# First chunk of an mLSTM kernel: another order of its pieces, smaller first feed-forward units, a weight quarter narrowed in halves, no spare products

## The chip, the cores and the metric

The kernel runs on one NeuronCore of a Trainium2 chip. The metric is the device time of one execution in microseconds (us), the median over executions; lower is better. The core has a matrix engine (PE, with its weight loads shown apart as PEld), a vector engine (DVE), an activation engine (ACT), a third elementwise engine (POOL), and a queue that issues most transfers (SP). Each engine works through its own list of instructions in order, and waits on counters (semaphores) that other engines raise.

## The reference

Two blocks follow each other. The first is an mLSTM cell over 4 batches, 8 heads, 768 steps, head size 40:

```python
for t in range(S):
    m_new = np.maximum(f_gate[:, :, t] + m, i_gate[:, :, t])
    f_stab = np.exp(f_gate[:, :, t] + m - m_new)
    i_stab = np.exp(i_gate[:, :, t] - m_new)
    C = f_stab * C + i_stab * einsum('bhd,bhe->bhde', vt, kt)
    n = f_stab * n + i_stab * kt
    h_tilde = einsum('bhde,bhe->bhd', C, qt)
    denom = max(abs(sum(n * qt)), 1.0)
    y[:, :, t] = sigmoid(o_gate[:, :, t]) * h_tilde / denom
```

Its output, as 3072 tokens of 320 values, goes through a feed-forward block with `w_in` of 320 x 2048 and `w_out` of 2048 x 320:

```python
h = x @ w_in
return np.maximum(0.01 * h, h) @ w_out
```

The two weights arrive as 64-bit floats and are narrowed to 32 bits on the chip.

## The kernel before, in words

The 768 steps are cut into 6 chunks of 128. Within a chunk the cell is computed without a loop over steps: scores of keys against queries, times a matrix of decays (`w`, the exponential of a masked sum), times values, plus a state that is carried from chunk to chunk. One *step* `s` is one batch in one chunk, `s = 4 * chunk + batch`, so chunk 0 holds s = 0 to 3 and chunk 1 holds s = 4 to 7. A chunk's four outputs are transposed into `xT`, and the feed-forward of that chunk (a *group*) runs on them while the next chunk's cell is worked out.

The feed-forward of group 0 comes in *units*. A first kind makes 2 x 128 of the 2048 hidden values from all 5 row blocks of `w_in` (`rows`, line 888) and applies the leaky ReLU on ACT (`relu`, 897). Pair `j` (0 to 7) needs quarter `j // 2` of `w_in`. A second kind, `part(n, m)` (923), multiplies a quarter `m` of the hidden values of batch `n` by `w_out`. In group 0 before the change, the first kind is cut in halves of two batches (`half`, 915), and units 0 and 1 belong to the first chunk's order; 14 halves and 16 parts follow, numbered 0 to 29. From group 1 on, a pair is one product over all four batches, cut in two units by row blocks (`pair`, 902).

`narrow_weights(n)` (235) is a generator of seven steps, one on ACT (the absolute value, line 246) and six on DVE (248 to 262). n = 0 to 3 are the quarters of `w_in`, 1280 columns each; n = 4 to 11 are eighths of `w_out`, 640 columns each.

The order of all this is written out by hand in two places, inside a context that keeps every engine's list as it was emitted:

- `ORDER` (1087) is a list for chunk 0. Its words are calls: `ld` loads k, q, v of a batch and `lo` its o gate; `lw` loads a piece of weights as raw 64-bit words; `g`, `ge`, `ug` are the gates of a chunk (scans on DVE, exponentials on ACT, transposes on PE); `tr` and `tc` transpose k or q on PE and copy them on ACT; `ab` and `abw` spread the gate sums over a matrix (PE) and add the mask (DVE, 456); `exp` is the exponential of `w` (ACT, 473); `vu` is v times a gate (POOL, 483); `sc` and `scm` the scores (PE, 578) and their product with `w` (DVE, 585); `st` and `stc` the state (PE, 593) and its copy (DVE, 601); `val` the values (PE, 658); `den` the denominators (DVE, 650 to 652); `o` the gate's tanh (ACT, 509); `gate` the gating (DVE, 670); `gp` the scaling (POOL, 687); `x` and `xc` the transposes to `xT` (PE, 861) and their copies (ACT, 874 and 875); `ps` clears what a state buffer needs (POOL, 160 to 162); `tiles` clears others; `nw n` is one step of narrowing; `ff` a feed-forward unit; `fd` and `ll` load for chunk 1. `warm 12` is 12 products of the identity with itself, whose result nobody reads.
- After that list, a loop over the 30 units of group 0 (1154). `PASSES[i]` says how many further steps of narrowing (w_in's third quarter onward) stand ahead of unit i; `fetch` at which unit the last pieces of `w_out` are asked for; `place` after which unit each of chunk 1's 13 cell pieces stands: the scores (`u_parts`, PE 635 and 640, DVE 645 and 617) and the outputs (`u_plain`, PE 698, DVE 650 to 709, POOL 687) of s = 4, 5, 6, one gate transpose, the same two of s = 7, and four times `u_x1`, the transposes of s = 4 to 7 into `xT` with their copies.

Then comes the first unit of group 1, which reads all four batches of `xT`. The buffers of products are two sets of four banks (`psf` for the feed-forward, the gate sums and `warm`; `psc` for the cell).

Of the kernel before, what the change touches and what calls it, by code (L numbers as in the profile page):

```python
# [20 lines left out]
def kernel(  # L21
# [27 lines left out]
    B, H, S, D = q.shape  # L49
    P = 128  # L50
# [15 lines left out]
    NF = FF // P  # L66
    GT = B * P
    KF = Dm // P
    KR = Dm - KF * P
    KC = Dm // DP  # L70
# [4 lines left out]
    gp = ctx.enter_context(tc.tile_pool(name="gates", bufs=1))  # L75
# [96 lines left out]
    def f_of(r, j):  # L172
        n, e = divmod(j, 2)
        return 4 * n + 2 * r + e

    def w_row(r, slot, j):
        n, e = divmod(j, 2)
        at = (2 * slot + e) * P
        return w_in[DP * r : DP * (r + 1), n, at : at + P]
# [3 lines left out]
    raws = {}  # L183
# [48 lines left out]
            rows = moe_w_out[2 * m * P : 2 * (m + 1) * P, :]  # L232
            nc.sync.dma_start(to.rearrange("p (a d) -> p a d", d=Dm), rows.rearrange("(a p) d -> p a d", p=P))

    def narrow_weights(n):

        if not wide:
            return  # L240
        raw, dst = raws.pop(n)
        words = raw.bitcast(U32).rearrange("p (c two) -> p c two", two=2)
        lo, hi = words[:, :, 0], words[:, :, 1]
        d = dst.bitcast(U32)
        low, top = lo.bitcast(F32), hi.bitcast(F32)
        nc.scalar.activation(dst, top, AF.Abs)
        yield
        nc.vector.tensor_scalar(
            dst, dst, scalar1=2.0**-15, scalar2=122879.9921875, op0=ALU.max, op1=ALU.min,
        )  # L250
        yield
        nc.vector.tensor_scalar(
            d, d, scalar1=0x07FFFFFF, scalar2=3, op0=ALU.bitwise_and, op1=ALU.logical_shift_left,
        )
        yield
        nc.vector.scalar_tensor_tensor(d, in0=hi, scalar=0xC0000000, in1=d, op0=ALU.bitwise_and, op1=ALU.bitwise_or)  # L256
        yield
        nc.vector.tensor_scalar(hi, d, scalar1=0xFF800000, scalar2=None, op0=ALU.bitwise_and)
        yield
        nc.vector.scalar_tensor_tensor(low, in0=lo, scalar=2.0**-52, in1=top, op0=ALU.mult, op1=ALU.mult)  # L260
        yield
        nc.vector.tensor_tensor(dst, dst, low, op=ALU.add)  # L262
# [78 lines left out]
    st = {}  # L341
# [540 lines left out]
    def by_slot(t, dt=F32):  # L882
        return t[:].bitcast(dt).rearrange("p b (k t) -> p k b t", t=P)

    def ff_units(g):
        xT = by_slot(st["xT", g])

        def rows(j, ph, cols, slots):
            bs = slice(cols.start // P, cols.stop // P)
            for slot in slots:  # L890
                for r in range(2):
                    nc.tensor.matmul(  # L892
                        ph[r][:, cols], lhsT=w_row(r, slot, j), rhs=xT[DP * r : DP * (r + 1), slot, bs, :],
                        start=(slot == 0), stop=(slot == KC - 1),
                    )

        def relu(j, ph, cols):
            for r in range(2):
                f = f_of(r, j)
                nc.scalar.activation(acts[:, f, cols], ph[r][:, cols], AF.Prelu, alpha=0.01)  # L900

        def pair(j):
            ph = []

            def first():
                ph.extend(psf.tile([P, GT], F32, name=f"ph{r}", tag="mm") for r in range(2))
                rows(j, ph, slice(0, GT), range(3))

            def second():
                rows(j, ph, slice(0, GT), range(3, KC))  # L910
                relu(j, ph, slice(0, GT))

            return [first, second]

        def half(j, h):
            ph = [psf.tile([P, GT], F32, name=f"ph{r}", tag="mm") for r in range(2)]
            cols = slice(h * GT // 2, (h + 1) * GT // 2)
            rows(j, ph, cols, range(KC))
            relu(j, ph, cols)

        po = {}

        def part(n, m):
            if m == 0:
                po[n] = psf.tile([P, Dm], F32, name="po", tag="mm")
            for f in range(m * NF // 4, (m + 1) * NF // 4):
                nc.tensor.matmul(  # L927
                    po[n][:], lhsT=acts[:, f, ts(n, P)], rhs=w_out[:, f, :], start=(f == 0), stop=(f == NF - 1),
                )
            if m == 3:  # L930
                if n < 2:
                    y = wk.tile([P, Dm], F32, name="y")[:]
                else:
                    y = wk.tile([P, H, D1], F32, name="hn")[:].rearrange("p h d -> p (h d)")[:, :Dm]
                nc.scalar.copy(y, po[n][:])
                nc.sync.dma_start(out[n * S + g * P : n * S + (g + 1) * P, :], y)

        if g == 0:

            ins = [(j, h) for j0 in range(0, NF // 2, 2) for h in range(2) for j in (j0, j0 + 1)]  # L940
            return [lambda j=j, h=h: half(j, h) for j, h in ins] + [
                lambda n=n, m=m: part(n, m) for m in range(4) for n in range(B)
            ]
        firsts = [u for j in range(NF // 2) for u in pair(j)]
        for n in range(2):
            firsts[KH + 2 * n] = lambda n=n, u=firsts[KH + 2 * n]: (u(), mix_early(n))
        return firsts, fast_units(g)
# [5 lines left out]
    def mix_early(n):  # L953

        nc.vector.tensor_tensor(s3_at[:, n], quarter(n, 0, 0), quarter(n, 1, 0), op=ALU.subtract)
# [91 lines left out]
    def run(steps, n=None):  # L1047

        for _ in range(H if n is None else n):
            next(steps, None)  # L1050
# [34 lines left out]
            nc.tensor.matmul(st["warm"][:], lhsT=ident[:], rhs=ident[:], start=True, stop=True)  # L1085

    ORDER = """
ld 0; warm 12; ld 1; ld 2; lo 0; lo 1; lo 2; lw 0
g 0; ld 3; lw 1; lw 2; lo 3; ge 0; ug 0; tr 0 0
tr 0 1; vu 1; vu 0; tc 0 0; ab 0; abw 0; tr 1 0; tc 0 1  # L1090
exp 0; sc 0; abw 1; tr 1 1; tc 1 1; st 0; tc 1 0; exp 1
st 1; scm 0; stc 1; stc 0; ab 2; tiles; g 1; abw 3
sc 1; scm 1; ge 1; abw 2; val 0; tr 2 0; tr 2 1; val 1
o 1; den 0; tc 2 1; gate 1; ps 1; tc 2 0; o 0; exp 2
gate 0; gp 0; ug 1; sc 2; scm 2; x 0; tr 3 0; nw 0
nw 0; vu 2; den 1; gp 1; nw 0; nw 0; nw 0; exp 3
tr 3 1; tc 3 0; ps 0; st 2; tc 3 1; xc 0; val 2; vu 3
sc 3; stc 2; nw 0; o 2; nw 0; nw 1; scm 3; den 2
x 1; xc 1; gate 2; st 3; o 3; gp 2; nw 1; nw 1
stc 3; nw 1; ff 0; val 3; den 3; x 2; gate 3; fd 4  # L1100
nw 1; ps 3; xc 2; ff 1; gp 3; x 3; nw 1; ll 4 1
xc 3; ps 2; ll 4 2; fd 5; ll 5 1; lw 3; lw 4; lw 5
lw 6; fd 6; fd 7; ll 5 2; nw 1
"""

    def first_chunk():

        ffs, narrow = [], {}

        def ff(n):  # L1110
            if not ffs:
                ffs.extend(ff_units(0))
            ffs[n]()

        def step(n):
            if n not in narrow:
                narrow[n] = narrow_weights(n)
            next(narrow[n], None)

        acts_of = {  # L1120
            "ld": load, "lo": load_o, "lw": load_weights, "g": gates, "ge": gates_exp, "warm": warm,
            "ug": lambda c: gates_T(c, bus[c][0] if c == 0 else bus.pop(c)[0]),
            "tr": u_transpose, "tc": transpose_copy, "ab": lambda n: spread_first(bus[0][1], n), "abw": spread_mask,
            "exp": lambda n: run(prep_exp(n)), "vu": prep_vu, "tiles": prepare_tiles, "sc": u_scores, "scm": scores_mix,
            "st": state, "stc": state_copy, "val": u_values, "den": values_den, "o": prep_o, "gate": gate,
            "gp": gate_scale, "nw": step, "ps": prepare_step, "x": u_x, "xc": x_copy, "ff": ff,
            "warmer": warmer, "idle": idle, "fd": feed, "ll": load_late,
        }
        for line in ORDER.split("\n"):
            for what in line.split(";"):  # L1130
                name, *args = what.split() or [None]
                if name:
                    acts_of[name](*map(int, args))
        return ffs

    E = mybir.EngineType
    with tc.manual_schedule(engines={E.PE, E.DVE, E.Activation, E.Pool}):
        ffs = first_chunk()[2:]
        fetch = {6: (3, 4), 17: (7,), 10: (5, 6)}
        PASSES = (3, 2, 1, 0, 3, 5, 3, 1, 0, 1, 4, 2, 3, 4, 1, 2, 8, 4, 5, 4, 5, 4, 0, 7, 3, 5, 5, 1, 2, 8)  # L1140
        place = (1, 4, 7, 9, 11, 15, 15, 18, 23, 25, 27, 27, 28)
        late = {}
        now = (None for n in range(2, QN + NF // 2) for _ in narrow_weights(n))

        def exps():
# [8 lines left out]
        for i in range(len(ffs)):  # L1154
            run(now, PASSES[i])
            for n in fetch.get(i, ()):
# [102 lines left out]
        for g in range(1, NB):  # L1259
            firsts, seconds = three_units(g, 0) if g in THREE else ff_units(g)  # L1260
            ffs = firsts + seconds
# [51 lines left out]
```

## Time and profile before

| | before |
|---|---|
| median of 3 executions | 491.95 us (491.8 to 493.19) |
| the profiled execution | 493.52 us, span 491.7 us, mean granted clock 0.975 |
| PE busy in the span | 480.2 us (98%) |
| DVE busy | 371.4 us (76%) |
| ACT busy | 197.2 us (40%) |
| POOL busy | 164.2 us (33%) |
| PE busy, 0 to 137.5 us | 129.20 us, DVE 120.14 us, mean granted clock 0.91 |
| PE busy, 137.5 to 371.6 us | 234.10 of 234.10 us |
| PE busy, 371.6 to 491.7 us | 116.89 of 120.1 us |

The span goes from the first instruction to the last. Everything that the change edits lies in the first 137.5 us. The ORDER list ends on PE at 48.1 us (the last transposes of batch 3), the units run from 49.07 to 136.92, and group 1 begins at 137.50. A row of the profile names line, engine, operation, the tile written and the tile read; a fp32 product shows as two rows. The granted clock is the share of full speed at which PE was let run.

### The profile page before, as it was taken

Reading aid. Unit: us, or ns where it says so; the run is one execution under the profiler, and the core shown is the slowest. Engines: PE = TensorE matmul, PEld = TensorE weight load, DVE = VectorE, ACT = ScalarE, POOL = GpSimd, SP = SyncE. Lnnn points to the kernel's source line nnn. Section 1 sums busy time; section 2 is a strip of 40 time slices with the busy share of each in tenths; the row PEclk is TensorE's granted clock in tenths of the full one; section 3 lists DMA queues with packets and bytes.
Section 4 is the critical chain, followed back from the end, with each engine's and each line's share of the span. In section 5 each row is a group of like instructions: output and inputs, shape, how many; then the busy total and the mean of one; then the engine's idle time right before and its main releaser. Section 6 shows DMA issues by size and latency. Waiting matters only on the chain.

```text
span 491.7 us, 12838 instructions
## 1 busy us (share of the span) xinstructions
PE 480.2 (98%) x5137; PEld 381.7 (78%) x5137; DVE 371.4 (76%) x595; ACT 197.2 (40%) x510; POOL 164.2 (33%) x207
## 2 busy tenths in 40 slices
PE   7989998999999999999999999999999999999997
PEld 7877887777745479985549995557998889988997
DVE  5797999989943999777898677779899968335611
ACT  4773884562453241324333141425023752156310
POOL 5233664270410624827280472635220002100020
PEclk9757999999999999999999999999999999999999
DMA  7867777897434477668687867876161030100001
GB/s 139 186 192 135 209 176 137 247 226 155 102 122 88 115 156 184 166 143 202 138 190 159 193 164 174 180 174 172 35 237 42 1 107 1 41 15 0 1 1 54
DMA packets 142699, 63.41 MB, mean 129 GB/s; under 512 B 110832, under 2 KB 130864, under 8 KB 142640
## 3 DMA queue, kind: packets, MB, share of 16 engines
q1 hardware_dynamic: 142256, 62.47, 53.0%
q8 instruction: 40, 0.66, 0.6%
q10 hardware_dynamic: 384, 0.13, 0.1%
q14 instruction: 19, 0.16, 0.1%
HBM read 51.68 MB, written 8.27 MB: 122 GB/s over the span
## 4 chain that ended last, share of the span: by engine, by line
PE 79%; DVE 11%; SPq 3%; DMA 2%; issue 2%; ACT 1%; POOL 1%; DVEq 0%; POOLq 0%
PE po L968 31%; PE ph L892 23%; PE ph L818 8%; PE pe L818 4%; PE pT L728 3%; PE sd L635 3%; DMA S<-in_v_dram 1%; DVE raw L260 1%; SPq L228 1%; DVE w_out L262 1%; PE warm L321 1%; PE po L927 1%; PE sc L578 1%; PE sd L640 1%; DVE w_out L256 1%
## 5 line engine op out<-in xcount | busy, mean ns | idle before, releaser
L892 PE MATMUL ph<-xT,w_in 64*128 64x512 f32 (+1 forms) x800 | 146.8, 516 | 0.6 <-ACT xT L874 0.6
L892 PEld LDWEIGHTS ph<-xT,w_in 64*128 64x128 f32 x800 | 77.9, 190 | 58.1 <-issue 50.8
L968 PE MATMUL po<-w_out,acts 128*128 128x160 f32 x640 | 91.0, 301 | 0.0
L968 PEld LDWEIGHTS po<-w_out,acts 128*128 128x128 f32 x640 | 87.5, 190 | 3.4 <-ACT w L473 1.5
L900 ACT ACTIVATE acts<-ph 128x512 f32<-128x512 f32 (+1 forms) x80 | 36.8, 508 | 85.2 <-PE ph L892 85.2
L613 POOL TENSOR_TENSOR S<-S,f 40x336 f32<-40x336 f32 x36 | 33.6, 933 | 92.7 <-PE pT L728 49.0
L473 ACT ACTIVATE w<-w,gT 128x64 f32<-128x64 f32 (+1 forms) x192 | 52.0, 348 | 30.3 <-POOL w L465 29.2
L968 PE MATMUL po<-raw,acts 128*128 128x160 f32 x320 | 45.1, 299 | 0.0
L968 PEld LDWEIGHTS po<-raw,acts 128*128 128x128 f32 x320 | 44.0, 190 | 0.0
L1001 POOL TENSOR_TENSOR y<-y,raw 128x160 f32<-128x160 f32 x10 | 5.5, 555 | 112.3 <-ACT y L1000 112.3
L645 DVE TENSOR_TENSOR qn<-w,sd 64x512 f32<-64x512 f32 x40 | 27.4, 684 | 19.4 <-PE sd L640 13.0
L840 DVE SCALAR_TENSOR_TENSOR acts<-ph,acts 128x512 f32<-128x512 f32 x32 | 20.6, 685 | 20.7 <-ACT acts L838 20.7
L927 PE MATMUL po<-w_out,acts 128*128 128x320 f32 x128 | 36.1, 436 | 0.0
L465 POOL TENSOR_TENSOR w<-w,i 128x512 f32<-128x512 f32 x20 | 33.9, 1697 | 0.1
L526 DVE TENSOR_TENSOR qn<-kqT,ea 64x512 f32<-64x512 f32 x32 | 33.1, 1033 | 1.0
L927 PEld LDWEIGHTS po<-w_out,acts 128*128 128x128 f32 x128 | 23.7, 190 | 9.7 <-DVE w_out L262 0.4
L742 POOL TENSOR_TENSOR xb<-xb,den 128x320 f32<-128x320 f32 x16 | 11.6, 727 | 48.7 <-DVE xb L739 48.7
L838 ACT ACTIVATE acts<-pe 128x512 f32<-128x512 f32 x32 | 17.4, 594 | 19.2 <-PE pe L818 19.0
L746 DVE STREAM_TRANSPOSE x<-xb 128x512 f32<-128x512 f32 x16 | 17.7, 1107 | 7.7 <-POOL xb L742 7.7
L844 ACT ACTIVATE acts<-acts 128x512 f32<-128x512 f32 x32 | 19.7, 633 | 8.0 <-DVE acts L840 8.0
L968 PE MATMUL po<-raw 128*128 128x160 f32 x160 | 22.7, 300 | 0.0
L635 PEld LDWEIGHTS sd<-kqT 40*64 40x64 f32 x640 | 19.7, 135 | 3.7 <-issue 3.0
(164 smaller groups left out, 786.4 us busy)
## 6 DMA issues: line engine op xcount, KB each, us to landing
w<-a_dr SPq DMA_DIRECT2D x40, 128.0 KB, 3.6
rb<-in_k_dram SPq DMA_DIRECT2D x64, 80.0 KB, 2.7
rb<-in_q_dram SPq DMA_DIRECT2D x64, 80.0 KB, 2.7
rb<-in_o_gate_dram SPq DMA_DIRECT2D x64, 80.0 KB, 2.7
xT<-x_dr SPq DMA_DIRECT2D x32, 160.0 KB, 3.2
ea<-a_dr SPq DMA_DIRECT2D x32, 128.0 KB, 3.3
x_dr<-x SPq DMA_DIRECT2D x16, 256.0 KB, 3.2
kn<-in_k_dram SPq DMA_DIRECT2D x24, 160.0 KB, 3.4
```

Of the source, the lines that this page charges most:

```text
L465: nc.gpsimd.tensor_tensor(w, w, cm2.unsqueeze(1).to_broadcast([P, H, SL]), op=ALU.add)
L473: yield nc.scalar.activation(w[:, h, :], w[:, h, :], AF.Exp, bias=gT[c][:, 0, bh : bh + 1], scale=1.0)
L526: nc.vector.tensor_tensor(mixed(s)[rows, 1 - r], d["kqT"][rows, 1].rearrange("p (h t) -> p h t", t=SL), d["ea"][rows], op=ALU.mult,)
L613: nc.gpsimd.tensor_tensor(new, old, g, op=ALU.mult)
L635: nc.tensor.matmul(bank[1 - u][toks, h, :], lhsT=kqT[rows, 0, ts(h, SL)], rhs=kqT[rows, 1, ts(h, SL)], start=True, stop=True,)
L645: nc.vector.tensor_tensor(mixed(s)[toks, u], w[toks], bank[1 - u][toks], op=ALU.mult)
L818: nc.tensor.matmul(ph[r][:], lhsT=parts["w", key][n][part, at : at + P], rhs=xs[key][part, slot, :], start=start and slot == 0, stop=stop ...
L840: nc.vector.scalar_tensor_tensor(fs[r], in0=ph[r][:], scalar=1.0 + EPS, in1=fs[r], op0=ALU.mult, op1=ALU.add,)
L892: nc.tensor.matmul(ph[r][:, cols], lhsT=w_row(r, slot, j), rhs=xT[DP * r : DP * (r + 1), slot, bs, :], start=(slot == 0), stop=(slot == KC ...
L900: nc.scalar.activation(acts[:, f, cols], ph[r][:, cols], AF.Prelu, alpha=0.01)
L927: nc.tensor.matmul(po[n][:], lhsT=acts[:, f, ts(n, P)], rhs=w_out[:, f, :], start=(f == 0), stop=(f == NF - 1),)
L968: nc.tensor.matmul(bank[:], lhsT=left[:, f, :], rhs=right[:, f, :], start=f == 0, stop=f == KH - 1)
```

## The change

Four things change, all in chunk 0 and group 0.

1. `ORDER` is another list of the same pieces. Loads of the o gate, the gates, the transposes and the narrowing stand in other places, and `warm 12` is left out.
2. The first units are `some(j, b0, b1)`, over any run of batches. Before, ORDER held two halves: pairs 0 and 1 over batches 0 and 1. Now it holds pair 0 over batch 0, pair 0 over batch 1, and pair 1 over batches 0 and 1. Of the 30 units behind the list, units 0 and 1 are pairs 0 and 1 over batches 2 and 3, units 2 to 13 are pairs 2 to 7 over all four batches, each cut in two by row blocks as in later groups, and units 14 to 29 are the parts as before.
3. `narrow_weights(n, e)` can take half of a quarter: e = 0 is the columns of the even pair, e = 1 those of the odd one. ORDER narrows quarter 0 in these halves, 640 columns per step.
4. `PASSES`, `fetch` and `place` have other numbers. In `place` the last five pieces, the outputs of s = 7 and the four transposes into `xT`, all have unit 29, the last one.

```diff
-    def narrow_weights(n):
+    def narrow_weights(n, e=None):
...
+        if e is not None:
+            lo, hi, dst = (a.rearrange("p (k e t) -> p e k t", k=KC, t=P)[:, e] for a in (lo, hi, dst))
...
-        def half(j, h):
+        def some(j, b0, b1):
+
             ph = [psf.tile([P, GT], F32, name=f"ph{r}", tag="mm") for r in range(2)]
-            cols = slice(h * GT // 2, (h + 1) * GT // 2)
+            cols = slice(b0 * P, b1 * P)
...
-            ins = [(j, h) for j0 in range(0, NF // 2, 2) for h in range(2) for j in (j0, j0 + 1)]
-            return [lambda j=j, h=h: half(j, h) for j, h in ins] + [
-                lambda n=n, m=m: part(n, m) for m in range(4) for n in range(B)
-            ]
+            ins = [lambda j=j: some(j, 2, B) for j in range(2)] + [u for j in range(2, NF // 2) for u in pair(j)]
+            return some, ins + [lambda n=n, m=m: part(n, m) for m in range(4) for n in range(B)]
...
     ORDER = """
-ld 0; warm 12; ld 1; ld 2; lo 0; lo 1; lo 2; lw 0
-g 0; ld 3; lw 1; lw 2; lo 3; ge 0; ug 0; tr 0 0
-tr 0 1; vu 1; vu 0; tc 0 0; ab 0; abw 0; tr 1 0; tc 0 1
-exp 0; sc 0; abw 1; tr 1 1; tc 1 1; st 0; tc 1 0; exp 1
-st 1; scm 0; stc 1; stc 0; ab 2; tiles; g 1; abw 3
-sc 1; scm 1; ge 1; abw 2; val 0; tr 2 0; tr 2 1; val 1
-o 1; den 0; tc 2 1; gate 1; ps 1; tc 2 0; o 0; exp 2
-gate 0; gp 0; ug 1; sc 2; scm 2; x 0; tr 3 0; nw 0
-nw 0; vu 2; den 1; gp 1; nw 0; nw 0; nw 0; exp 3
-tr 3 1; tc 3 0; ps 0; st 2; tc 3 1; xc 0; val 2; vu 3
-sc 3; stc 2; nw 0; o 2; nw 0; nw 1; scm 3; den 2
-x 1; xc 1; gate 2; st 3; o 3; gp 2; nw 1; nw 1
-stc 3; nw 1; ff 0; val 3; den 3; x 2; gate 3; fd 4
-nw 1; ps 3; xc 2; ff 1; gp 3; x 3; nw 1; ll 4 1
-xc 3; ps 2; ll 4 2; fd 5; ll 5 1; lw 3; lw 4; lw 5
-lw 6; fd 6; fd 7; ll 5 2; nw 1
+ld 0; g 0; ld 1; lo 1; ge 0; lo 0; tr 0 0; ld 2
+lw 0; ug 0; tr 0 1; ab 0; tr 1 0; ld 3; tc 0 0; tc 0 1
+vu 0; sc 0; lw 1; tr 1 1; abw 0; abw 1; exp 0; lo 3
+vu 1; tc 1 1; st 0; st 1; tc 1 0; sc 1; tr 2 0; ab 2
+scm 0; val 0; tr 2 1; stc 1; exp 1; tiles; o 0; scm 1
+tc 2 1; lo 2; g 1; gate 0; vu 2; abw 2; lw 2; den 0
+vu 3; val 1; ge 1; abw 3; stc 0; o 1; st 2; ps 0
+tc 2 0; stc 2; ug 1; ps 1; nw 0 1; nw 0 0; exp 2; sc 2
+gp 0; tr 3 0; tr 3 1; nw 0 0; den 1; gate 1; tc 3 1; scm 2
+nw 0 1; tc 3 0; gp 1; nw 0 1; x 0; sc 3; exp 3; val 2
+xc 0; ps 2; nw 0 0; nw 0 0; nw 0 1; nw 0 0; x 1; nw 1
+o 2; nw 0 1; nw 0 0; nw 0 0; st 3; o 3; ff 0 0 1; scm 3
+nw 0 1; den 2; fd 4; ll 4 1; nw 1; val 3; gate 2; nw 0 1
+lw 3; lw 4; gp 2; xc 1; fd 5; nw 1; gate 3; ff 0 1 2
+ll 4 2; nw 1; den 3; nw 1; gp 3; x 2; nw 1; ll 5 1
+xc 2; stc 3; ff 1 0 2; x 3; lw 5; ps 3; nw 1; fd 6
+xc 3; fd 7; lw 6; ll 5 2
 """
...
-        fetch = {6: (3, 4), 17: (7,), 10: (5, 6)}
-        PASSES = (3, 2, 1, 0, 3, 5, 3, 1, 0, 1, 4, 2, 3, 4, 1, 2, 8, 4, 5, 4, 5, 4, 0, 7, 3, 5, 5, 1, 2, 8)
-        place = (1, 4, 7, 9, 11, 15, 15, 18, 23, 25, 27, 27, 28)
+        fetch = {10: (5, 6), 16: (7,), 4: (3, 4)}
+        PASSES = (6, 1, 2, 0, 1, 0, 4, 1, 0, 4, 3, 2, 9, 0, 1, 3, 11, 11, 1, 0, 5, 12, 2, 0, 2, 2, 2, 4, 0, 7)
+        place = (1, 5, 6, 9, 10, 12, 16, 20, 29, 29, 29, 29, 29)
```

The rest of the diff passes the new arguments through `ff` and `nw`.

More of the change, by code (lines that the diff above doesn't have):

```diff
@@ L233, in load_weights @@
             nc.sync.dma_start(to.rearrange("p (a d) -> p a d", d=Dm), rows.rearrange("(a p) d -> p a d", p=P))
-    def narrow_weights(n):
+    def narrow_weights(n, e=None):
         if not wide:
             return
-        raw, dst = raws.pop(n)
+        raw, dst = raws[n]
         words = raw.bitcast(U32).rearrange("p (c two) -> p c two", two=2)
         lo, hi = words[:, :, 0], words[:, :, 1]
+        if e is not None:
+            lo, hi, dst = (a.rearrange("p (k e t) -> p e k t", k=KC, t=P)[:, e] for a in (lo, hi, dst))
         d = dst.bitcast(U32)
@@ L1108, in first_chunk, with ff, step @@
         ffs, narrow = [], {}
-        def ff(n):
+        def ff(j, b0, b1):
             if not ffs:
                 ffs.extend(ff_units(0))
[L1113 to L1118, printed above, removed]
+            ffs[0](j, b0, b1)
+        def step(n, e=None):
+            if (n, e) not in narrow:
+                narrow[n, e] = narrow_weights(n, e)
+            next(narrow[n, e], None)
         acts_of = {
@@ L1133, in first_chunk @@
                     acts_of[name](*map(int, args))
-        return ffs
+        return ffs[1]
     E = mybir.EngineType
     with tc.manual_schedule(engines={E.PE, E.DVE, E.Activation, E.Pool}):
-        ffs = first_chunk()[2:]
-        fetch = {6: (3, 4), 17: (7,), 10: (5, 6)}
-        PASSES = (3, 2, 1, 0, 3, 5, 3, 1, 0, 1, 4, 2, 3, 4, 1, 2, 8, 4, 5, 4, 5, 4, 0, 7, 3, 5, 5, 1, 2, 8)
-        place = (1, 4, 7, 9, 11, 15, 15, 18, 23, 25, 27, 27, 28)
+        ffs = first_chunk()
+        fetch = {10: (5, 6), 16: (7,), 4: (3, 4)}
+        PASSES = (6, 1, 2, 0, 1, 0, 4, 1, 0, 4, 3, 2, 9, 0, 1, 3, 11, 11, 1, 0, 5, 12, 2, 0, 2, 2, 2, 4, 0, 7)
+        place = (1, 5, 6, 9, 10, 12, 16, 20, 29, 29, 29, 29, 29)
         late = {}
```

## The prediction

> **What bounds the kernel now.** I read the engine totals first, then busy time by stretch, since a share of the whole span mixes stages.
>
> ```profile
> PE 480.2 (98%) x5137; PEld 381.7 (78%) x5137; DVE 371.4 (76%) x595; ACT 197.2 (40%) x510; POOL 164.2 (33%) x207
> ```
>
> PE is nearly full. The change ends where chunk 1's feed-forward begins, so the stretches up to there count. The columns are stretch and length, then busy PE, PEld, DVE, ACT and POOL, granted clock, DMA share, GB/s.
>
> ```profile
> 8.97:46.23 37.26, 33.32 (x294) 28.81 (x295) 30.47 (x67) 22.90 (x61) 11.43 (x25) 0.68 0.79 176
> ...
> 51.30:128.07 76.77, 74.46 (x1079) 59.78 (x1075) 72.27 (x101) 42.38 (x112) 31.64 (x27) 1.00 0.80 189
> 49.07:136.92 87.85, 85.54 (x1137) 67.70 (x1130) 83.08 (x113) 51.30 (x133) 41.21 (x34) 1.00 0.76 178
> ```
>
> From the first unit that covers batches 2 and 3 (49.07) to chunk 0's last product (136.92) PE idles 87.85 - 85.54 = 2.31 us. DVE, which narrows the weights, idles 4.5 of 76.77 us. Two engines run close together, so an early start pays only if both have it. Before 49 us the waits and the clock count:
>
> ```profile
> 14.00:16.00 2.00, 2.00 (x34) 1.77 (x36) 1.88 (x7) 1.30 (x5) 0.00 (x0) 0.50 0.86 195
> 16.00:18.00 2.00, 2.00 (x25) 1.88 (x25) 1.86 (x8) 1.15 (x5) 0.00 (x0) 0.96 0.64 167
> 24.00:26.00 2.00, 2.00 (x16) 1.78 (x15) 0.63 (x2) 2.00 (x5) 1.30 (x3) 0.50 0.49 107
> 42.00:44.00 2.00, 2.00 (x14) 1.53 (x10) 0.33 (x1) 0.66 (x2) 0.00 (x0) 0.63 0.39 61
> ```
>
> PE runs at half clock from 13 to 16.6 and from 23.4 to 43.9 us. DVE's waits from 8 to 50 us:
>
> ```profile
> DVE den L650 <- PE pa L658: 2.7, 1, 2.7
> DVE w L456 <- PE ab L446: 2.0, 1, 2.0
> DVE w L585 <- PE sc L578: 1.6, 1, 1.6
> DVE S L601 <- PE dC L593: 0.9, 1, 0.9
> DVE x L670 <- PE pa L658: 0.7, 1, 0.7
> ```
>
> Last, the border to chunk 1, on ACT and PE (start, duration):
>
> ```profile
> 134.28 0.38 PE L861 MATMUL xt<-ident,hn 128*128 128x128 f32 x2
> ...
> 134.49 0.27 PE L862 MATMUL xt<-ident,hn 128*64 128x128 f32 x1
> ...
> 134.60 2.32 PE L927 MATMUL po<-w_out,acts 128*128 128x320 f32 x8
> ...
> 136.98 0.47 ACT L874 COPY xT<-xt 64x384 f32<-64x384 f32 x1
> 137.47 0.37 ACT L875 COPY xT<-xt 64x256 f32<-64x256 f32 x1
> ```
>
> Here PE transposes batch 3's x (`xt`) ahead of one more product, and ACT's copies pass partly beneath it. PE waits from 136.92 to 137.50, and its first unit of chunk 1 takes 5.01 instead of 4.49 us, being paced by the copies: 0.58 + 0.52 = 1.10 us.
>
> **The change, part by part.**
>
> *No spare products, other order: the start-up.* The 12 products (24 rows, 1.47 to 6.5) stand on nobody's path: `tg` needs ACT's `bu`, done at 6.45. What they do is raise the clock by the time work comes: four transposes at 8.82 take 0.66 us and at 26.29, at half clock, 1.06; 32 rows of `ab` take 1.17 at 7.71 and 2.09 at 13.73. At half clock `tg` also stands behind four transposes now; the first mask addition on DVE moves from 8.97 to about 10.1 (0.9 of `ab`, 0.2 of the transposes): +1.1.
>
> By the Trainium skill (TensorE: Matmul & The Clock Gate, "What's actually happening") the clock is halved by default and a busy window of about 3.4 us releases it. By that rule the removed products cost one such window, and the trace's 5 us of spare products before full clock agree; the 1.1 us above stands without it.
>
> DVE's work up to batch 3's denominators stays the same (`stc 3` moves behind them, `gate 3` ahead, 0.68 each) except for the halved narrowing of w_in's first quarter. Uncontended rows at 640 columns take 0.48, 0.49, 0.83, 0.49, 0.83, 0.82 (L248 to L262), 3.94 in sum; at 1280 columns 0.81, 0.78, 1.49, 0.81, 1.48, 1.49, or 6.86. Two halves: 7.88, so +1.0. On ACT two absolute values of 0.80 replace one of 1.39.
>
> DVE's five waits above total 7.9; the 2.0 is part of the start, 5.9 lie after 8.97. What is late next, followed through the new queues: `stc 1` behind the state products (0.35 to 1.15), `scm 1` behind `exp 1` (1.2), `gate 0` behind batch 0's values (0.1 to 1.35), `gate 3` behind batch 3's (0.6 to 2). The last is shorter than the 2.7, since 128-column units now stand ahead of these products in place of one of 256 columns (20 rows, 4.64 us at half clock). The low ends hold at full clock (values 1.98 for 16 rows), the high ends at half (3.64). Sum 2.25 to 5.7, against 5.9: -3.65 to -0.2. A 128-column unit has no row; it costs at most its 256-column one, 2.43 at full clock, at least half of that, and lies inside these waits.
>
> Start-up sum: 1.1 + 1.0 - 3.65 = -1.55, or 1.1 + 1.0 - 0.2 = +1.9. Following PE alone (units over batch 0, over batch 1, then both, behind these waits) gives -2.5 to +1.6. I take -0.2, nearer the half-clock end for the early part and the full-clock end for the late part: first full unit at 48.9.
>
> SP: `lo 1` and `lo 0` go ahead of `ld 2` (two issues of 0.87), which is not needed before 16. The first and second quarter are issued 0.87 sooner, the third 0.87 later. The fourth quarter's ten issues and w_out's first go ahead of `fd 5` and `ll 5`, some 7 us later for batch 1 of chunk 1, whose transposes come at 66. POOL: `vu 3` now waits for its load (landing about 24.4) ahead of `ps 0`, `ps 1` and `gp 0`; `x 0` on PE stands behind that, and `sc 3` behind `x 0`, at about 29, when `exp 3` is running anyway. These cost nothing while they hold; if the load is late, all of it shifts.
>
> *Units of chunk 0.* 512-column rows take 4.49 per 20, two halves 2 x 2.26: no change. Of PE's 2.31 idle, 0.74 + 0.97 at 79 to 81 (`hN` behind ACT and behind DVE's L617) goes: the second such product now follows unit 9, at about 77, and L617 is done by 75. Late next: the first `hN`, because L260 and L262 of the third quarter (3.0 to 3.8) go ahead of its L645; 0 to 0.5. And w_out: DVE's remaining work of 5.0 + 72.27 less the last cell's block, now behind (1.40 + 0.50 + 1.29 + 1.39 = 4.58), gives 72.7; with 4 of idle from about 46 this ends at 123, when PE reaches the last quarter of the products (48.9 + 83.1 - 9.1). Sum: -1.0; ends -2.0 and +1.5.
>
> *The border.* `place` puts the last cell's `hN` and all four transposes behind unit 29. PE's queue then reads: 36 products without a break, `hN` (1.06), four `xt` (0.33 each). Copies of one batch take 1.72 (132.36 to 134.08). First copy 1.06 + 0.52 (126.70 to 127.22) = 1.58 after the last product; the last batch's begins 3 x 1.72 = 5.16 later; its first is done at 7.21, and PE resumes at 7.26; pacing 0.52: 7.78. The last cell's gate (1.2 on DVE) and scale (0.74 on POOL) pass under the first three batches' copies. The 1.06 + 4 x 0.33 = 2.4 was done inside the 85.54 before, and 1.10 was lost: 7.78 - 2.4 - 1.10 = +4.3. Its cover was the products that used to follow each transpose. Nothing in the queues can shorten it; ends 4.0 and 4.6, plus the clock, below.
>
> **Sum.** -0.2 - 1.0 + 4.3 = +3.1. After the border PE's queue is the same, at full clock. The profiled execution took 493.52 (span 491.7), 1.57 above the median of 491.95: 496.6 against it, 495.05 against the median.
>
> **Rivals.**
> - *The start-up wins more than the border costs.* All of DVE's new waits at their low ends (PE at full clock by 10 us) and PE never waiting for w_out: -2.5 - 2.0 + 4.0 = -0.5. DVE with no wait at all would give 1.1 + 1.0 - 5.9 = -3.8, and -1.8 in sum: 490.2. It decides if full-size units begin before 46.3. For it: `o` loads come before the weights, where the trace shows ACT 2.7 late. Against it: half clock in 24 of the 37 us.
> - *A tie.* Start-up -2, units -1.5, border +4.3: +0.8, 492.8.
> - *The border also halves the clock.* Between the last `xt` and the restart PE idles some 2.6 us, around it only small products. The trace halves the clock after the stretch from 16.6 to 23.4, with such work and 0.7 idle, but not after 78 to 84.9 with 1.7 idle. One window of 3.4 us at half clock loses 1.7: 495.05 + 1.7 = 496.8. The same page ("HAM oscillation") warns of idle gaps over 3.4 us, which would leave this one alone.
> - *The start-up stays at half clock* and w_out comes late: +1.6 + 1.5 + 4.3 = +7.4, 499.4.
>
> **Chances.** The forecast +1.5 to +4.5: 0.42; halved clock or half-clock start-up, +4.5 and more: 0.22; the tie: 0.16; the win: 0.20, because a dozen small waits are worked by hand. About 0.3% (1.5 us) is what a measurement of this kernel can tell. Faster 0.20, same 0.16, slower 0.64. Range 490.8 to 498.5, from within the win to within the slow start-up.
>
> **What would show it.** Right: 36 products in one block, then 16 copies on ACT, PE resuming some 7.3 us behind them; PE's wait at 79 gone; first mask addition at 10. Wrong: the first full-size unit before 46.3 or after 51; or PE waiting for w_out longer than 2 us.

## The result, and the profile after

| | before | after |
|---|---|---|
| median | 492.94 us of 6 (491.8 to 493.8) | 503.9 us of 6 (502.43 to 505.26) |
| ratio to before | | 1.0226, 95% interval 1.02 to 1.0251 |
| span of the profiled execution | 491.7 us | 501.3 us |
| mean granted clock | 0.975 | 0.966 |

The change makes the kernel 2.3% slower, about 11 us; the forecast was +3.1 us, and its range ended at 498.5. The two profiled spans differ by 9.6 us, and all of it arises before the first 60 rows of chunk 1's feed-forward end. Four executions of the variants below (500.12, 508.42, 700 and 808.72 us) and one of the kernel before (1237.86) ran in a slower state; they count in the medians given, not in the ratios. The stretch answering to 49.07:136.92 of before comes first, from the first full-size unit over batches 2 and 3 to the end of the last product, and then a part of it (columns as before: stretch, length, busy PE, PEld, DVE, ACT, POOL, granted clock, DMA share, GB/s).

```profile
50.18:138.68 88.50, 85.62 (x974) 55.31 (x970) 69.13 (x101) 43.64 (x102) 27.58 (x26) 0.96 0.72 164
74.40:81.20 6.80, 6.69 (x72) 3.88 (x74) 4.87 (x9) 1.08 (x3) 1.53 (x2) 0.51 0.64 168
```

The stretch begins 1.11 us later. It is 0.65 longer, although 2.4 us of work (the last cell product and the four transposes) has left it: like for like +3.05. For 6.8 us in its middle, from 74.2 to 81.0, PE ran at half clock; before, the clock was full throughout. PE's waits from 45 to 155 us (engine, line, waited for: total, times, longest) say where:

```profile
PE sd L640 <- POOL vu L493: 2.9, 2, 2.5
PE ph L892 <- ACT xT L874: 1.9, 1, 1.9
PE xt L861 <- ACT xT L875: 1.5, 1, 1.5
PE xt L861 <- POOL hn L687: 0.9, 1, 0.9
```

The first took 0.2 before; the other three are the border. DVE's L617 and ACT's L900, which held up `hN` at 79 to 81 before, are gone, and PE waits nowhere for `w_out`. On PE and POOL in time (start, duration, engine, line, operation, tiles; in brackets the idle time before and what ended it) the first reads:

```profile
65.96 1.13 PE L698 MATMUL hN<-S,qn 128*64 128x42 f32 x32
...
68.05 2.85 PE L892 MATMUL ph<-xT,w_in 64*128 64x512 f32 x12
...
74.51 0.36 PE L640 MATMUL sd<-S,vu 64*40 64x42 f32 x3 [2.47 <-POOL vu L493]
...
76.31 8.61 PE L892 MATMUL ph<-xT,w_in 64*128 64x512 f32 x28
```

```profile
68.55 0.74 POOL L687 TENSOR_TENSOR x<-x,den 128x320 f32<-128x320 f32 x1 [0.57 <-DVE x L709]
69.25 1.31 POOL L502 TENSOR_TENSOR y<-rb,gT 128x320 f32<-128x320 f32 x1
70.63 1.89 POOL L613 TENSOR_TENSOR S<-S,f 40x336 f32<-40x336 f32 x1
72.60 1.85 POOL L493 TENSOR_TENSOR vu<-kn,gT 128x320 f32<-128x320 f32 x1
```

Between one batch's outputs (`hN`, s = 4) and the next batch's scores (`sd`, s = 5) POOL has four steps to do, one behind the other, that end at 74.45. PE now has one unit (12 rows, 2.85 us) to do meanwhile. Before, it had the three units that `place` put between them:

```profile
64.84 7.04 PE L892 MATMUL ph<-xT,w_in 64*128 64x256 f32 x60
...
73.25 0.30 PE L640 MATMUL sd<-S,vu 64*40 64x42 f32 x3 [0.24 <-POOL vu L493]
```

Even there PE waited 0.24 us for the same `vu`: that chain had no slack to give. At the end of the new wait (74.2) the clock drops, and the next 28 rows take 8.61 us; at full clock, in the trace below that fills this wait, the same 28 take 6.28.

The border, on PE and on ACT (first and last of the 16 copies):

```profile
138.60 1.13 PE L698 MATMUL hN<-S,qn 128*64 128x42 f32 x32
...
142.02 0.44 PE L861 MATMUL xt<-ident,hn 128*128 128x128 f32 x2 [1.48 <-ACT xT L875]
...
143.49 0.44 PE L861 MATMUL xt<-ident,hn 128*128 128x128 f32 x2 [0.92 <-POOL hn L687]
...
145.97 15.22 PE L892 MATMUL ph<-xT,w_in 64*128 64x512 f32 x60 [1.94 <-ACT xT L874]
```

```profile
140.25 0.47 ACT L874 COPY xT<-xt 64x384 f32<-64x384 f32 x1
...
146.82 0.37 ACT L875 COPY xT<-xt 64x256 f32<-64x256 f32 x1
```

PE restarts 7.29 us after its last product. ACT copies without a break from 140.25 to 147.19, so the copies set the restart. From 145.9 to 149.3 the clock is at half, and the first 60 rows of chunk 1 take 15.22 us against 14.01 before. The end of those rows minus the end of the last product is 22.51 us, against 14.59 before; less the 2.4 of work that moved here, that is +5.5.

So the 9.6 us of the two profiles are +1.1 (start), +3.05 (units) and +5.5 (border).

### The profile page after: what moved, and what is told of

Its sections match the earlier page's. It is cut to its first block, busy times and chain, and to the rows that moved or that the text cites. A ratio compares the mean times of both kernels' runs of the same rounds, so it can differ in the third digit from the quotient of the medians.

```text
span 501.3 us, 12592 instructions
## 1 busy us (share of the span) xinstructions
PE 482.6 (96%) x5013; PEld 370.4 (74%) x5013; DVE 367.7 (73%) x601; ACT 195.6 (39%) x501; POOL 160.0 (32%) x207
## 4 chain that ended last, share of the span: by engine, by line
PE 87%; SPq 3%; DMA 3%; ACT 2%; DVE 2%; POOL 2%; issue 1%; POOLq 0%; ACTq 0%
PE po L967 31%; PE ph L892 25%; PE ph L818 7%; PE po L928 7%; PE pe L818 4%; PE pT L728 3%; PE sd L635 3%; PE sc L578 1%; DMA kn<-in_k_dram 1%; SPq L228 1%; PE sd L640 1%; PE pa L658 1%; PE tkq L563 1%; ACT xT L874 1%; DMA S<-in_v_dram 1%
## 5 line engine op out<-in xcount | busy, mean ns | idle before, releaser
L892 PE MATMUL ph<-xT,w_in 64*128 64x512 f32 (+2 forms) x700 | 151.1, 581 | 1.9 <-ACT xT L874 1.9
L892 PEld LDWEIGHTS ph<-xT,w_in 64*128 64x128 f32 x700 | 69.3, 200 | 69.7 <-issue 64.1
L900 ACT ACTIVATE acts<-ph 128x512 f32<-128x512 f32 (+2 forms) x70 | 35.4, 558 | 97.1 <-PE ph L892 97.1
L613 POOL TENSOR_TENSOR S<-S,f 40x336 f32<-40x336 f32 x36 | 33.1, 919 | 99.7 <-PE pT L728 45.3
L645 DVE TENSOR_TENSOR qn<-w,sd 64x512 f32<-64x512 f32 x40 | 27.4, 684 | 20.0 <-PE sd L640 9.2
L465 POOL TENSOR_TENSOR w<-w,i 128x512 f32<-128x512 f32 x20 | 31.8, 1590 | 7.9 <-DMA w<-a_dr 7.8
L838 ACT ACTIVATE acts<-pe 128x512 f32<-128x512 f32 x32 | 17.4, 595 | 19.1 <-PE pe L818 19.0
L640 PE MATMUL sd<-S,vu 64*40 64x42 f32 x576 | 20.4, 219 | 2.9 <-POOL vu L493 2.9
```

The costliest lines, as they stand in the source:

```text
L465: nc.gpsimd.tensor_tensor(w, w, cm2.unsqueeze(1).to_broadcast([P, H, SL]), op=ALU.add)
L613: nc.gpsimd.tensor_tensor(new, old, g, op=ALU.mult)
L640: nc.tensor.matmul(dC[u][:, h].rearrange("p k d -> p (k d)"), lhsT=d["ku"][toks, h], rhs=S_v[s % NL][toks, u, h, :, :V1], start=True, stop ...
L645: nc.vector.tensor_tensor(mixed(s)[toks, u], w[toks], bank[1 - u][toks], op=ALU.mult)
L892: nc.tensor.matmul(ph[r][:, cols], lhsT=w_row(r, slot, j), rhs=xT[DP * r : DP * (r + 1), slot, bs, :], start=(slot == 0), stop=(slot == KC ...
```

## The experiments

The kernel before ran beside each group, with medians of 492.48 to 492.98. Times below are medians, ratios are to that kernel, and "us" worked out from a ratio are the ratio less 1 times 493.

### The border alone, undone and done

The tail of `place` in the changed kernel, moved back ahead of the last products:

```diff
-        place = (1, 5, 6, 9, 10, 12, 16, 20, 29, 29, 29, 29, 29)
+        place = (1, 5, 6, 9, 10, 12, 16, 20, 25, 26, 27, 27, 28)
```

> The changed kernel with one edit: the last cell's outputs and the four transposes stand behind units 25, 26, 27, 27 and 28 again, between products. Border theory: of the 11.0 us lost, the border holds 7.26 + half clock (1.3) less the 2.4 of products it only moves and the 0.6 lost before, about 5.5; so PE's gap at the border falls from 7.3 to about 1 us, no half clock at 146 us, and the time falls from 503.9 to about 498.4. Rival (DVE would be late there anyway, since it ends its narrowing at 127.7 and only then turns to the last cell): PE waits in front of the last cell's outputs instead, and less than 2 us come back: 502.

Measured: 496.42 us, ratio 1.0077 (1.0052 to 1.0103). PE passes the border without a gap, and the wait for POOL stays as it was:

```profile
138.86 2.32 PE L928 MATMUL po<-w_out,acts 128*128 128x320 f32 x8
141.11 13.47 PE L892 MATMUL ph<-xT,w_in 64*128 64x512 f32 x60
```

The last five places are worth 7.3 us of the 11 (ratio 1.0226 less 1.0077), more than the forecast's 4.3 plus the 1.10 that before lost at its own border. The two traces, from the first full-size unit to the end of the first 60 rows of chunk 1, differ by 6.5 us (111.0 and 104.5), well within what the two intervals allow; 4.3, 1.1 and the 1.2 of clock found below make 6.6. The other way round, the kernel before with only the tail of `place` as changed:

```diff
-        place = (1, 4, 7, 9, 11, 15, 15, 18, 23, 25, 27, 27, 28)
+        place = (1, 4, 7, 9, 11, 15, 15, 18, 29, 29, 29, 29, 29)
```

> The kernel before with one edit: the last five pieces of chunk 1's cells (outputs of the last step, four transposes) stand behind the last unit, 29. Border theory: PE resumes 7.3 us behind the last product, 4.3 us more than before, and a half-clock window follows, 1.3: 492.9 becomes 497 to 498.5. Rival (the cost belongs to the new order of the start and not to the border): under 1.5 us, 494.

Measured: 500.55 us, ratio 1.0157 (1.0136 to 1.0178): +7.7 us, above what was expected. Its trace shows why the border costs more than its idle time: the clock is at half from 139.9 to 146.8, and the first 60 rows are slow.

```profile
133.81 1.13 PE L698 MATMUL hN<-S,qn 128*64 128x42 f32 x32
...
139.52 0.44 PE L861 MATMUL xt<-ident,hn 128*128 128x128 f32 x2 [1.75 <-POOL hn L687]
...
141.18 16.35 PE L892 MATMUL ph<-xT,w_in 64*128 64x512 f32 x60 [1.11 <-ACT xT L874]
```

```profile
PE po L927 <- DVE w_out L262: 1.0, 1, 1.0
```

The restart stands 7.37 us after the start of the last cell product, as in the changed kernel. From the end of that product to the end of the 60 rows it takes 23.65 us against 14.59 before; less the 2.4 of work that moved, that is +6.7. Another 1.0 is a wait for `w_out` at 125, which the kernel before does not have. Together they come to the 7.7 of the medians.

### The clock at the border

If the half clock comes from PE's idle time, products of the identity that nobody reads should keep it full without moving the restart.

```diff
+                if fn is u_plain and s == 2 * B - 1:
+                    warmer()
+                if fn is u_x1:
+                    idle({5: 12, 6: 7, 7: 14}.get(s, 0))
```

`warmer` takes a product buffer, and `idle(n)` makes n products of the identity in it.

> The changed kernel with spare products of the identity (nobody reads them) behind the last cell product (12) and between the last four transposes (12, 7 and 14), so that PE is not idle at the border. It keeps the copies and the restart where they are. Theory: a share of the border's 7.5 us is the clock, lost because PE idles; with PE busy the clock stays full after 146, the first unit of chunk 1 goes as fast as its copies allow, and 1.0 to 2.5 us come back: 501.5 to 503. Rival 1: the first units are paced by the copies on ACT, at half clock or full, and nothing comes back: within 0.7 of the changed kernel. Rival 2: spare products delay the transposes and their copies: slower by 1 or more.

Measured: 502.52 us, ratio 1.0194 (1.0157 to 1.0231). The clock stayed full, but the fill was too long: the last of these products ended at 145.85, behind the last copy (145.04), so they set the restart themselves. That trace cannot say what the clock alone is worth. With shorter fills (6, 3 and 7):

> The changed kernel with spare products of the identity (nobody reads them) between the last transposes, 6, 3 and 7, sized by their measured 0.236 us each to end before the copies that PE waits for; the longer row of 12, 7 and 14 had ended behind the last copy. Theory: the copies decide the restart, 7.4 us after the start of the last cell product as in the changed kernel, and only the half clock of 146 to 149 goes away: the first 60 rows of chunk 1 take 13.4 to 14 us in place of 15.2, and the time falls by 1.2 to 1.8, to 502.1 to 502.7. Rival: the border's 7.5 us are the copies alone; the clock stays but the rows wait for copies, within 0.6 of the changed kernel.

Measured: 502.43 us, ratio 1.0198 (1.018 to 1.0217).

```profile
137.44 1.13 PE L698 MATMUL hN<-S,qn 128*64 128x42 f32 x32
...
144.81 14.01 PE L892 MATMUL ph<-xT,w_in 64*128 64x512 f32 x60 [0.38 <-ACT xT L874]
```

The restart stands where it stood, 7.37 us after the start of the last cell product; the half clock is gone, and the 60 rows take 14.01 instead of 15.22. The theory held in the trace: of the border about 1.2 us is clock that idling PE loses, and the rest is waiting for copies. The medians point the same way, 1.4 us by the two ratios, but their intervals overlap.

### The wait for POOL, and the clock behind it

First a try that missed, the pieces of chunk 1 spaced wider, with the border left in place:

```diff
-        place = (1, 5, 6, 9, 10, 12, 16, 20, 29, 29, 29, 29, 29)
+        place = (1, 5, 8, 10, 12, 13, 16, 20, 29, 29, 29, 29, 29)
```

> The changed kernel with one edit: chunk 1's second and third cells stand two or three units behind the outputs of the cell before them (place 1, 5, 8, 10, 12, 13 in front of the rest, which is as in the changed kernel). POOL theory: POOL needs some 6 us after a cell's outputs (scale, q by its gate, state, k by its gate) before the next cell's products can run; with one unit between, PE waits 2.5 and 0.4 us, and the idle window halves the clock from 74.4 to 81.2, 3.4 us more. Expected: both waits and the half clock at 74 gone, about 6 us less: 498. Rival (the clock falls because of the many small products, not because of the wait): only the 2.9 us of waits come back, 501, and the half clock stays.

Measured: 506.32 us, ratio 1.028 (1.0255 to 1.0305), slower than the change. The wait for POOL shrank to 0.6 and the half clock at 74 went, as the theory had it, but the next pair of pieces (scores at 12, outputs at 13) now stood too close:

```profile
PE hN L698 <- DVE qn L645: 3.5, 1, 3.5
```

DVE reached L645 at 96.14, behind eleven narrowing steps of `w_out`, and the clock went to half from 98.5 to 101.9. Spacing moved the wait from one pair to the next, and from POOL to DVE. In this trace the border also ran 6.8 us at half clock (146.3 to 153.1) instead of 3.4. The old places, but with the changed units and the changed narrowing:

```diff
-        place = (1, 5, 6, 9, 10, 12, 16, 20, 29, 29, 29, 29, 29)
+        place = (1, 4, 7, 9, 11, 15, 15, 18, 25, 26, 27, 27, 28)
```

> The changed kernel with the places of chunk 1's cell pieces of before, but for the ninth (25 in place of 23): 1, 4, 7, 9, 11, 15, 15, 18, 25, 26, 27, 27, 28. With the last five pieces moved back alone it took 496.4. My theory (two losses, both made by places: the border, about 7.5 us, and the product of scores waiting for POOL at 72 to 75 with the half clock behind it) expects that PE's wait for POOL there falls under 0.5 us, that the clock stays full from 48 to 137, and 496.4 - 2.5 - 1 to 3 = 491 to 494. The rival, that the order of narrowing (PASSES) and not the places makes PE wait, expects that the wait only moves, to the second scores or to a cell product waiting for DVE, as it did with the wide spacing: 496 or more.

Measured: 493.76 us, ratio 1.0029 (1.0008 to 1.005). The wait for POOL and the border are both gone. So `place` carries nearly all of the loss: 11.1 - 1.4 = 9.7 us. The early places are 2.4 of it (ratio 1.0077 less 1.0029), the tail the other 7.3. The profiled execution (495.59, above its median) shows a wait of another kind, of which more below; so the 2.4 is the difference of two sets of places, not the price of the one wait. Next, is it the wait or the clock behind it? On top of the first experiment (tail moved back):

```diff
+                if fn is u_parts and s == B + 1:
+                    warmer()
+                    idle(9)
                 fn(s)
```

> The changed kernel with its last five places moved back to 25, 26, 27, 27 and 28 (496.4 by itself), and 9 spare products (2.1 us) ahead of the second scores of chunk 1, where PE waits 2.65 us for POOL at 72 to 75. The scores still start when POOL is done; only PE's idle time is filled. Theory: the half clock of 74.5 to 81.3 comes from that idle time, costs 3.4 us, and goes: 493 to 494. Rival 1: it comes from the mix of small products, or by chance, and stays: 496 to 497. Rival 2: the spare products delay the transposes of q behind them, so the wait only moves behind them: 496 or more.

Measured: 495.09 us, ratio 1.0048 (1.003 to 1.0066), against 1.0077 without the fill. PE fills the time in which it waited, and the scores start when POOL is done:

```profile
72.11 2.27 PE L1084 MATMUL warm<-ident 128*128 128x128 f32 x18
...
75.75 0.30 PE L640 MATMUL sd<-S,vu 64*40 64x42 f32 x3 [0.22 <-POOL vu L493]
...
76.83 6.28 PE L892 MATMUL ph<-xT,w_in 64*128 64x512 f32 x28
```

The stretch from the first full-size unit to group 1 without the fill:

```profile
50.05:141.11 91.06, 88.00 (x1017) 57.23 (x1011) 78.06 (x113) 49.76 (x118) 36.24 (x33) 0.96 0.69 160
```

and with it, up to group 1 and over the former half-clock period:

```profile
51.47:139.37 87.90, 87.26 (x1034) 57.91 (x1028) 77.56 (x112) 49.71 (x118) 35.93 (x33) 1.00 0.71 160
74.40:81.20 6.80, 6.58 (x116) 4.04 (x118) 4.86 (x8) 4.13 (x10) 2.77 (x2) 1.00 0.34 66
```

No half clock is left in the stretch, and it is 3.16 us shorter, close to the 3.4 expected, though PE does no useful work in the fill. In these two executions the clock behind the wait (3.16) cost more than the wait (2.65). By the medians the gain is smaller, 1.4 us (ratios 1.0077 and 1.0048, with intervals that overlap), and 495.09 lies outside the 493 to 494 that was expected. Part of that is that this loss was not the same size in every execution: with the same wait of 2.5 us the trace of the shortened border fill shows 3.4 us at half clock instead of 6.8. Part may lie in the start-up, which is 1.4 us later in this trace (51.47 against 50.05); one trace each does not say.

### The start-up

The kernel before without its 12 spare products:

```diff
-ld 0; warm 12; ld 1; ld 2; lo 0; lo 1; lo 2; lw 0
+ld 0; ld 1; ld 2; lo 0; lo 1; lo 2; lw 0
```

> The kernel before with one edit: the 12 spare products are left out (their result is read by nothing). Prediction's price: first mask addition 1.1 us later (half clock until about 9.6 us), which passes through to the end or is taken up by DVE's later waits: 0 to +1.1, 493 to 494. Rival (the clock falls into another pattern for the whole start): the first full-size unit moves by more than 2 us either way.

Measured: 494.25 us, ratio 1.0035 (1.0016 to 1.0054): the spare products are worth 1.7 us (0.8 to 2.7) in the old list. Then the new list alone, in the kernel before (new `ORDER` with `some` and the halved narrowing; the other units, `PASSES`, `fetch` and `place` old):

```diff
-ld 0; warm 12; ld 1; ld 2; lo 0; lo 1; lo 2; lw 0
...
+ld 0; g 0; ld 1; lo 1; ge 0; lo 0; tr 0 0; ld 2
...
-            ins = [(j, h) for j0 in range(0, NF // 2, 2) for h in range(2) for j in (j0, j0 + 1)]
...
+            ins = [lambda j=j, h=h: some(j, 2 * h, 2 * h + 2) for j0 in range(0, NF // 2, 2) for h in range(2) for j in (j0, j0 + 1)][2:]
```

> The kernel before with the new list for chunk 0 alone (other order, no spare products, pair 0 over one batch each time, w_in's first quarter in halves); units, fetches, narrowing and places as before. Theory: first full-size unit some 1 us later, and the rest as before: 493.5 to 495. Of it the missing spare products are 1.3 (the kernel before without them took 494.25), so the order itself is worth between -1 and +1. Rival: the later start leaves DVE late for w_out and PE waits at 120 to 137: 496 or more. Other rival: the order wins by itself, the border and the places took it away: under 492.

Measured: 494.35 us, ratio 1.0029 (1.0008 to 1.0051). The list as a whole costs 1.4 us, about what leaving out the spare products costs by itself; its new order neither won nor lost anything that shows. It has the same ratio as the changed kernel with the old places, so with the old places the new units, narrowing counts and fetches cost nothing measurable. Undoing the list in the changed kernel, with pairs 0 and 1 over batches 0 and 1 as before:

```diff
-ld 0; g 0; ld 1; lo 1; ge 0; lo 0; tr 0 0; ld 2
...
-xc 3; fd 7; lw 6; ll 5 2
+ld 0; warm 12; ld 1; ld 2; lo 0; lo 1; lo 2; lw 0
...
+stc 3; nw 1; ff 0 0 2; val 3; den 3; x 2; gate 3; fd 4
+nw 1; ps 3; xc 2; ff 1 0 2; gp 3; x 3; nw 1; ll 4 1
+xc 3; ps 2; ll 4 2; fd 5; ll 5 1; lw 3; lw 4; lw 5
+lw 6; fd 6; fd 7; ll 5 2; nw 1
```

> The changed kernel with the list for chunk 0 undone (the old order, 12 spare products, pairs 0 and 1 over batches 0 and 1 in one unit each, w_in's first quarter narrowed whole); the 30 units, their fetches, narrowing and places stay as changed. Theory: the list is worth +1.1 us (first full-size unit 50.18 against 49.07), so this comes out 0.5 to 2 us faster than the changed kernel, with the waits for POOL and the border as they were: 502 to 503.4. Rival: the new list also set off the wait at 72 to 75 (its narrowing ends elsewhere and shifts DVE and ACT), and undoing it takes that away: 499 to 501.

Measured: 507.25 us, ratio 1.0304 (1.0267 to 1.0341): not faster, but 3.8 us slower than the changed kernel. Neither theory had this. PE's and ACT's waits show it:

```profile
PE ph L892 <- ACT acts L900: 3.8, 1, 3.8
```

```profile
ACT w_in L246 <- DMA raw<-in_moe_w_in_dram: 6.9, 1, 6.9
```

The changed `PASSES` puts the absolute value of `w_in`'s fourth quarter (L246) ahead of unit 1's ReLU in ACT's list. The old list loads that quarter (`lw 3`) at its end, issued from 49.5 to 58.1, and ACT has it at 60.4; the new list issues it from 42.4 to 49.5. ACT waits for it with the ReLU queued behind, and PE waits for the ReLU to free a buffer. The clock goes to half after this wait (63.5 to 66.9) and again with the one for POOL (77.2 to 84.0), and at the border for 6.8 us where it was 3.4. So the list and the units' numbers depend on each other, and a part of the change taken out by itself is not its price.

### A version that might beat both

The trace of the changed kernel with the old places showed this wait, and half clock from 101.4 to 108.2 right behind it:

```profile
PE tg L327 <- DVE hn L709: 2.2, 1, 2.2
```

DVE had 13 narrowing steps ahead of L709 in its list. Four were moved later:

```diff
-        PASSES = (6, 1, 2, 0, 1, 0, 4, 1, 0, 4, 3, 2, 9, 0, 1, 3, 11, 11, 1, 0, 5, 12, 2, 0, 2, 2, 2, 4, 0, 7)
+        PASSES = (6, 1, 2, 0, 1, 0, 4, 1, 0, 4, 3, 2, 9, 0, 0, 0, 15, 11, 1, 0, 5, 12, 2, 0, 2, 2, 2, 4, 0, 7)
```

> The changed kernel with the places 1, 4, 7, 9, 11, 15, 15, 18, 25, 26, 27, 27, 28 (493.8 by itself; its trace shows PE waiting 2.2 us for DVE's L709 at 99 to 101, with 13 steps of narrowing ahead of it in DVE's list, and half clock from 101.7 to 108.9), and four steps of narrowing moved from units 14 and 15 to unit 16. Theory: DVE reaches L709 some 2.6 us sooner, the wait goes and the half clock with it: 489.5 to 492. Rival: DVE's list is full, the wait comes back for w_out or for the scores of the last batch: 493 or more.

Measured: 494.3 us, ratio 1.0026 (1.0011 to 1.004). The wait fell to 0.4 and the half clock is not in this trace, but PE now waits for `w_out` at 128, and the median is where it was:

```profile
PE po L928 <- DVE w_out L262: 1.4, 1, 1.4
```

The rival's wait is there: narrowing put off at unit 16 comes due at `w_out`. That the median did not fall although the trace lost a wait and its half clock fits with the earlier trace having been one of the slower executions (495.59 against a median of 493.76). With the 12 spare products put back at the head of the list as well (`ld 0; warm 12; g 0` in place of `ld 0; g 0`):

> The same with the 12 spare products of the kernel before back at the head of the list. Theory: they are worth 1.3 to 1.7 us (the kernel before without them took 494.25), so 488 to 490.5, ahead of both kernels. Rival: with the new list the gates wait longer anyway and the clock is lost at 23 us as before; no difference to the kernel without them.

Measured: 495.08 us, ratio 1.0052 (1.0034 to 1.007): no gain; the loss of 1.3 us against the run before is within the overlap of their intervals. In this list the spare products did not help; the trace has half clock from 12.3 to 19.1 and from 22.5 to 49.8. None of the versions beats the kernel before.

## Why the prediction was wrong, point by point

The sign was right (0.64 on slower), the size was not: +3.1 forecast, +9.6 by the profiles and +11.1 by the ratio, beyond the range. The signs that the prediction named did not tell: those of being right came (PE restarts 7.29 us behind the last product, the wait at 79 is gone, the first mask addition at 9.86), and neither of being wrong did (the first full-size unit at 50.18, no wait of PE for `w_out`). They tested the rows that it had followed, and the one that failed was not among them.

- **"Units of chunk 0", -1.0 (bounds -2.0 and +1.5): measured +3.05. This is the step that failed.** What it said goes did go (`hN`'s waits at 79 to 81), and what it named as late next (`hN` behind DVE, then `w_out`) was not late. It listed only the neighbours of the pieces that had been waiting. `place` also moved the outputs of s = 4 from unit 4 to 5 and the scores of s = 5 from 7 to 6, and the prediction did not follow POOL through that: L687, L502, L613 and L493, 5.9 us from 68.55 to 74.45, with one unit in place of three to cover them. The profile of before had the warning, PE's 0.24 us of waiting for that same `vu`. PE's idle time in the stretch, forecast to fall from 2.31 by 1.0, is 2.88 us, all of it in two waits for `vu` (2.47 and 0.41). The half clock behind the first lost another 3.16 in the pair of traces that isolates it. The early places as a whole are worth 2.4 in the medians; how single executions make that up, with half clock of different length and the waits that the old places bring, stays open.
- **"The border", +4.3: measured +5.5 in the profiles, 7.3 to 7.7 by medians.** The mechanism was right to a few hundredths: restart expected 7.26 us after the last product, seen at 7.29, set by 16 copies on ACT. What the sum lacked was the clock. "The border also halves the clock" stood as a rival with +1.7; it happened, for 3.4 us as it assumed in the changed kernel (1.2 us, shown by filling PE's idle time) and for 6.8 us in the kernel before with the same tail. The 5.5 and the medians do not measure the same: the 7.3 also holds the 1.10 that before loses at its border, and the 7.7 the longer half clock and 1.0 of waiting for `w_out`.
- **"Start-up", -0.2 (bounds -2.5 and +1.9): measured +1.1 in the profiles, +1.4 (0.4 to 2.5) by medians.** Within its bounds. The first mask addition came at 9.86 (about 10.1 forecast). The first full unit came at 50.18 (48.9 forecast): the half clock lasted until 46.9 where before it ended at 43.5 (the prediction's edges of the clock before, 13 to 16.6 and 23.4 to 43.9, lie 0.3 to 0.4 too late), and DVE's wait for batch 3's values was 3.2 us where 2 was the upper end. DVE's waits after the first addition sum to 4.8, against 5.9 before: a saving of 1.1, where the -0.2 needs one of 2.3. The 128-column units, which had no row, took 2.5 us at half clock, about the upper bound given for full clock.
- **The clock in the sums.** Half clock had one chance in five, at the border or at the start. It came at the border (1.2) and in the units (3.16), on top of a wait that was not in the sum; that is the larger part of the 6.5 us between the forecast and the profiles.
- The cited rule of the Trainium skill (TensorE: Matmul & The Clock Gate, "HAM oscillation"), idle gaps over about 3.4 us, would have left the border alone. The traces disagree: at the border gaps of 0.92 and 1.94 with one batch's transposes between them were enough, and in the units one gap of 2.47.

## What to carry to other kernels

When pieces are placed closer together, follow the chain between them through every engine and add up its queue; a wait of 0.2 us in the profile is a chain without slack, not a free one. A wait of two or three microseconds on PE can cost as much again in clock behind it, so price a new PE wait with the half clock that may follow, and test that price by filling the wait with products nobody reads. Numbers tuned together (orders, counts of background steps, load times) should be undone together or one position at a time: half of a set may be worse than either whole.

## What the runs showed of the hardware

- The half clock came in steps of about 3.4 us: 3.4 (145.9 to 149.3), 6.8 (74.2 to 81.0), 20.5 (23.0 to 43.5 before). In the trace of the changed kernel its edges from 23.0 to 149.3 lie 7, 8, 2, 19 and 1 such lengths apart. By the Trainium skill (TensorE: Matmul & The Clock Gate, "What's actually happening") activity is watched in a free-running window of 3.4 us; these lengths agree.
- Counted in the 3.4 us ahead of each drop, PE was idle for 1.87 to 2.80 us at all twelve drops between 50 and 160 us in the fourteen traces (2.17 and 2.78 in the changed kernel, 2.22 with the old places). In the other stretches of 3.4 us on the same steps, at full clock, it was idle for 1.76 at most (1.71 at 77.6 to 81.0 before). That holds for this kernel's mix of products; no run tested a threshold. Before 50 us, among small products, the clock also fell with 0.06 to 1.42 us of idle time, so idle time is not all that counts there.
- How long it stays is not settled by the wait: behind the same wait of 2.5 us it was 6.8 us in the changed kernel and 3.4 with the shortened border fill, and behind the same tail of `place` 3.4 in one trace and 6.8 in three.
- The same program does not always get the same clock. With the new list the first full unit came between 50.05 and 51.47 in seven traces of the changed kernel and its variants with nothing different up to there, and at 47.72 in one, where the half clock ended at 38.8 instead of 46.7 to 48.8. The old list gave 49.07 in the kernel before and 47.36 in the one with only its tail of `place` changed. A difference of 3 us before 50 us between two single traces is therefore no evidence on a change to the start-up; the medians are.
